# Seventy identity products in TensorE's first gaps instead of twenty-four, in the bank of the second MLP's sum

## The chip, the cores and the metric

The kernel runs on one core of a Trainium2 chip. The metric is the device time of one execution in microseconds (us), as the median of several runs. The engines are called PE (TensorE), DVE (VectorE), ACT (ScalarE), POOL (GpSimd) and SP (SyncE, which issues the DMAs here).

## The reference

12288 queries of 128 channels attend to 768 keys, which are 4x4 averages of `kv` times `w_sr` and serve as values too. Two MLPs with 2048 hidden channels follow.

```python
kv_pool = kv.reshape(B, H // r, r, W // r, r, C).mean(axis=(2, 4))
k = v = kv_pool.reshape(B, -1, C) @ w_sr
a = softmax(q @ k.T / sqrt(C));  x = a @ v
h = x @ w_in;  x = (relu(h) ** 2) @ w_out
h = x @ w_in2
P = a[0] + a[1]*h + a[2]*h**2 + a[3]*h**3
Q = 1 + |b[0]|*|h| + |b[1]|*h**2
out = (P / (Q + 1e-6)) @ w_out2
```

## The kernel before, in words

The queries are cut into 25 blocks: one of 384 columns, 22 of 512, one of 384 and one of 256. Each block goes through three stages, and the stages of several blocks overlap.

- **Setup.** SP loads `kv` in 16 pieces; POOL (L486) and DVE (L482) sum them into pooled keys. PE projects them in two halves (L507 for the keys, L522 for the values); ACT (L511) and DVE (L515) split the projected keys into a high and a low part. The weights arrive as 64-bit words. DVE decodes each piece in four steps (L574, L582, L587, L592), and ACT and POOL split it.
- **Attention.** For each 128 queries PE makes the scores in six passes (L679), DVE takes the minimum, ACT the exponential, POOL the division (L697). PE transposes the result (L720), ACT and DVE split it, and PE multiplies by the values (L749 to L753).
- **First MLP.** The block's input is split into `xh` and `xl` (L779 or L782, and L785). For each of 16 hidden tiles PE makes three passes (L805 to L807, on `w0h` and `w0l`), ACT or DVE takes the ReLU (L847, L850), ACT or POOL the square, and PE adds to the block's sum `y1` (L819, or L823 to L825, on `w0o`, `w0oh`, `w0ol`). At the end `y1` is split into `yh` and `yl` (L779 or L782, and L785).
- **Second MLP.** Hidden tiles go in pairs, eight pairs a block. PE makes three passes for each tile (L805 to L807, on `w1h` and `w1l`). Then a chain of elementwise steps: ACT takes the absolute value (L944) and a square (L958), DVE a product for each tile (L960), POOL or ACT the denominator (L947 and L949, or L952), ACT a logarithm and an exponential (L969, L970), DVE three steps for the pair (L982, L984, L987). Of some pairs the result is split (L997 or L998, and L1000). PE adds to the sum `y2` (L819, or L823 to L825, on `w1o`, `w1oh`, `w1ol`). ACT scales it (L1020) and SP stores it (L1024).

The order of the work is not written out. Every step is given to a planner (`Plan.op`) with an urgency, a cost, the engine or engines that may do it, what it reads and writes, and what storage it takes. `Plan.order` plays all steps through once with these costs. An engine that is free takes the most urgent step that is ready and whose storage is free. The instructions are then issued in that order, on each engine one behind the other. So one more step on one engine can change the order of everything that follows on all of them. The eight banks of PSUM are shared by kinds of tiles, and `caps` says how many of each kind may be held: six of `st` (transposes and projections) and one of `y2`, the second MLP's sum.

The identity products (`warm`, L494 to L501) multiply the 128x128 identity by itself. Nothing reads what they give. They carry an urgency of 1e6, the last of all, so the planner places them where PE has nothing else that is ready.

Of the kernel before, what the change touches and what calls it, by code (L numbers as in the profile page):

```python
# [21 lines left out]
PE, ACT, DVE, POOL, DMA = "PE", "ACT", "DVE", "POOL", "DMA"  # L22
# [45 lines left out]
    rg=1,  # L68
    low=4,
    avs=5,  # L70
    warm=24,
    head=[384],
    tail=[384, 256],
    off=dict(
# [51 lines left out]
    warm=0,  # L126
# [242 lines left out]
def program(ctx, tc, CFG, fast, co, room, wsr, qT, kvT, w1_in, w1_out, w2_in, w2_out, outT):  # L369
# [30 lines left out]
    tiles = {}  # L400
# [5 lines left out]
    def mk(tag, key, shape=None, dtype=None):  # L406
        if tag in caps:
            tiles[key] = psum[:, P.slot[key], :]
            return tiles[key]
        if tag in RINGS:  # L410
            n = turn[tag] = turn.get(tag, -1) + 1
            in_room, at = place_of[tag, n % bufs[tag]]
            t = (room if in_room else more)[:, at:at + RINGS[tag]]
            if dtype:
                t = t.bitcast(dtype)
            if shape:
                size = 1
                for x in shape[1:]:
                    size *= x
                t = t[:, 0:size]  # L420
            else:
                shape = big.get(tag, [128, TM])
            if len(shape) == 3:
                t = t.rearrange("p (a b) -> p a b", b=shape[2])
            tiles[key] = t
            return t
        t = pools[tag].tile(shape or big.get(tag, [128, TM]), dtype or dts.get(tag, F32), tag=tag, name=tag)
        tiles[key] = t
        return t
# [20 lines left out]
    P = Plan(CFG)  # L450
# [25 lines left out]
    for c in range(0, NKEY, KC):  # L476
# [11 lines left out]
        if half(c):  # L488
            P.op(P0, (POOL, c_pool(KC * R2 // 2), add2, 0), wr=[("kv", c)])
        P.op(P0, (DVE, c_dve(KC * R2 // (2 if half(c) else 1)), go2, 0),  # L490
             new=[("const", ("poolT", c))] + ([] if c else [("o", "pool")]), rd=[("kv", c)] + (["pool"] if c else []))
    dma(P0, sizes[0] * 512, load_q(0), new=[("qr", ("qr", 0))])

    def warm(i):  # L494
        def go():
            o = mk("st", "warm") if i == 0 else tiles["warm"]
            nc.tensor.matmul(out=o[:, 0:128], lhsT=ident, rhs=ident, start=True, stop=True)
        return go
    for i in range(CFG["warm"]):
        P.op(1e6, (PE, 260.0, warm(i), 0), new=[("st", "warm")] if i == 0 else [],  # L500
             rd=["ident"], wr=["warm"] if i else [])  # L501

    for h in range(2):
# [575 lines left out]
def attn_moe_moe(  # L1079
# [79 lines left out]
    with tc.If(fits > 0) as branch:  # L1159
        with ExitStack() as c:  # L1160
            co = dict(c=c1(co_f, 0), nd=c1(co_f, 1), e=c1(v, 0), k1=c1(co_f, 2), k2=c1(co_f, 3), dp=c1(co_f, 4),
                      da=c1(co_f, 5), out=c1(co_f, 6))
            program(c, tc, SQUARES, True, co, *args)
    with branch.Else():
        with ExitStack() as c:
            co = dict(a=co_g[:, 0:4], e=c1(co_g, 0), b=co_g[:, 4:6], qc=c1(co_g, 6))
            program(c, tc, TERMS, False, co, *args)
# [39 lines left out]
```

## Time and profile before

| | |
|---|---|
| median of 3 runs | 1488.0 us (1486.13 to 1488.52) |
| the profiled execution | 1486.91 us |
| its span, first to last instruction | 1484.7 us |
| PE busy | 1439.5 us, 97% of the span |
| ACT, DVE, POOL busy | 1393.4, 1386.9, 1334.1 us |
| mean granted clock of PE | 0.989 |

The span is the time between the first and the last instruction in the trace; the execution's own time is 2.2 us longer. The granted clock is a share of full speed: 1.00 is 2.4 GHz and 0.50 is 1.2 GHz. A busy PE is not PE at its peak, since the ends of matmuls are modelled and they overlap.

### The profile page before, as it was taken

Reading aid. Unit: us, or ns where it says so; the run is one execution under the profiler, and the core shown is the slowest. Engines: PE = TensorE matmul, PEld = TensorE weight load, DVE = VectorE, ACT = ScalarE, POOL = GpSimd, SP = SyncE. Lnnn points to the kernel's source line nnn. Section 1 sums busy time; section 2 is a strip of 40 time slices with the busy share of each in tenths; the row PEclk is TensorE's granted clock in tenths of the full one; section 3 lists DMA queues with packets and bytes.
Section 4 is the critical chain, followed back from the end, with each engine's and each line's share of the span. In section 5 each row is a group of like instructions: output and inputs, shape, how many; then the busy total and the mean of one; then the engine's idle time right before and its main releaser. Section 6 shows DMA issues by size and latency. Waiting matters only on the chain.

```text
span 1484.7 us, 18746 instructions
## 1 busy us (share of the span) xinstructions
PE 1439.5 (97%) x5991; PEld 1053.8 (71%) x5991; DVE 1386.9 (93%) x1857; ACT 1393.4 (94%) x2318; POOL 1334.1 (90%) x1021
## 2 busy tenths in 40 slices
PE   5999999999999999999999999999999999999986
PEld 4887767766767777776777777777777777767764
DVE  7999999999999999999999999999989899989998
ACT  3789989999999999999999999999999999999996
POOL 4789999998999899999998997989999999889984
PEclk8999999999999999999999999999999999999998
DMA  7310000000000000000000000000000000000000
GB/s 283 114 36 8 13 0 15 14 2 8 15 8 15 8 3 13 15 8 8 8 15 8 1 15 15 8 8 15 8 8 8 8 13 1 11 5 3 8 8 12
DMA packets 15549, 28.62 MB, mean 19 GB/s; under 512 B 1745, under 2 KB 6737, under 8 KB 15441
## 3 DMA queue, kind: packets, MB, share of 16 engines
q1 hardware_dynamic: 15440, 27.34, 5.5%
q8 instruction: 49, 0.80, 0.2%
q14 instruction: 60, 0.48, 0.1%
HBM read 21.04 MB, written 6.29 MB: 18 GB/s over the span
## 4 chain that ended last, share of the span: by engine, by line
PE 67%; POOL 13%; ACT 8%; DVE 7%; issue 3%; DMA 1%; SPq 0%; POOLq 0%; ACTq 0%; DVEq 0%
PE psum L819 17%; PE psum L805 9%; PE psum L806 8%; PE psum L807 8%; PE psum L679 4%; PE psum L824 4%; POOL room L949 4%; PE psum L825 4%; PE psum L823 4%; PE psum L720 4%; POOL gL L871 3%; POOL room L947 2%; POOL room L856 2%; PE psum L750 1%; PE psum L749 1%
## 5 line engine op out<-in xcount | busy, mean ns | idle before, releaser
L949 POOL TENSOR_TENSOR room<-room 128x1024 f32<-128x1024 f32 (+2 forms) x150 | 348.3, 2322 | 3.6
L871 POOL TENSOR_TENSOR gL<-room,gH 128x512 fp32r<-128x512 f32 (+2 forms) x250 | 313.0, 1262 | 20.8 <-PE psum L824 15.8
L960 DVE SCALAR_TENSOR_TENSOR room<-room,cf,psum 128x512 f32<-128x512 f32 (+2 forms) x400 | 279.5, 720 | 17.4 <-ACT room L958 15.8
L819 PE MATMUL psum<-room,w1o 128*128 128x512 f32 (+2 forms) x600 | 285.2, 583 | 4.0 <-DVE room L987 4.0
L856 POOL TENSOR_TENSOR room<-room 128x512 f32<-128x512 f32 (+2 forms) x261 | 262.3, 1022 | 12.5 <-ACT room L847 6.6
L982 DVE SCALAR_TENSOR_TENSOR room<-room,v,psum 128x1024 f32<-128x1024 f32 (+2 forms) x200 | 246.1, 1232 | 21.2 <-ACT psum L970 19.4
L958 ACT ACTIVATE room<-psum,cf 128x512 f32<-128x512 f32 (+2 forms) x400 | 262.8, 688 | 0.0
L969 ACT ACTIVATE room<-room,cf 128x1024 f32<-128x1024 f32 (+2 forms) x200 | 226.3, 1132 | 25.4 <-POOL room L949 24.8
L984 DVE SCALAR_TENSOR_TENSOR psum<-room,cf,psum 128x1024 f32<-128x1024 f32 (+2 forms) x200 | 247.5, 1238 | 0.0
L987 DVE SCALAR_TENSOR_TENSOR room<-psum,room 128x1024 f32<-128x1024 f32 (+2 forms) x200 | 235.2, 1177 | 3.1
L944 ACT ACTIVATE room<-psum 128x512 f32<-128x512 f32 (+2 forms) x400 | 223.4, 593 | 12.5 <-PE psum L807 6.5
L947 POOL TENSOR_SCALAR room<-room,cf 128x1024 f32<-128x1024 f32 (+2 forms) x150 | 164.7, 1098 | 48.3 <-ACT room L944 36.0
L970 ACT ACTIVATE psum<-room 128x1024 f32<-128x1024 f32 (+2 forms) x200 | 202.7, 1015 | 0.7 <-DVE room L960 0.3
L805 PE MATMUL psum<-yh,w1h 128*128 128x512 f32 (+2 forms) x400 | 191.2, 478 | 4.8 <-DVE room L987 3.5
L805 PE MATMUL psum<-xh,w0h 128*128 128x512 f32 (+2 forms) x400 | 182.8, 457 | 1.6 <-DVE xh L782 1.2
L819 PEld LDWEIGHTS psum<-room,w1o 128*128 128x128 f32 x600 | 111.1, 192 | 63.1 <-issue 42.9
L806 PE MATMUL psum<-xl,w0h 128*128 128x512 f32 (+2 forms) x400 | 153.4, 383 | 1.5 <-DVE xl L785 1.2
L807 PE MATMUL psum<-yh,w1l 128*128 128x512 f32 (+2 forms) x400 | 154.2, 386 | 0.0
L806 PE MATMUL psum<-yl,w1h 128*128 128x512 f32 (+2 forms) x400 | 153.9, 385 | 0.0
L807 PE MATMUL psum<-xh,w0l 128*128 128x512 f32 (+2 forms) x400 | 153.6, 384 | 0.0
L847 ACT ACTIVATE room<-psum 128x512 f32<-128x512 f32 (+2 forms) x255 | 148.3, 601 | 5.1 <-PE psum L807 3.2
L865 ACT ACTIVATE gH<-room 128x512 fp32r<-128x512 f32 (+2 forms) x250 | 149.8, 632 | 2.9 <-POOL room L856 2.6
(126 smaller groups left out, 3124.4 us busy)
## 6 DMA issues: line engine op xcount, KB each, us to landing
room<-in_kv_dram SPq DMA_DIRECT2D x16, 384.0 KB, 7.8
room<-in_q_dram SPq DMA_DIRECT2D x22, 256.0 KB, 2.6
out_dram<-room SPq DMA_DIRECT2D x22, 256.0 KB, 2.0
room<-in_moe_w_in_dram SPq DMA_DIRECT2D x8, 512.0 KB, 4.6
room<-in_moe_w_out_dram SPq DMA_DIRECT2D x16, 256.0 KB, 2.7
room<-in_q_dram SPq DMA_DIRECT2D x2, 192.0 KB, 4.7
out_dram<-room SPq DMA_DIRECT2D x2, 192.0 KB, 1.9
room<-in_q_dram SPq DMA_DIRECT2D x1, 128.0 KB, 2.0
```

The costliest lines, as they stand in the source:

```text
L805: nc.tensor.matmul(out=out, lhsT=w_hi[m][:, sl], rhs=hi, start=True, stop=False)
L806: nc.tensor.matmul(out=out, lhsT=w_hi[m][:, sl], rhs=lo, start=False, stop=False)
L807: nc.tensor.matmul(out=out, lhsT=w_lo[m][:, sl], rhs=hi, start=False, stop=True)
L819: nc.tensor.matmul(out=o, lhsT=w_o[m][:, place[m][fi], :], rhs=rhs(), start=first, stop=last)
L856: nc.gpsimd.tensor_tensor(out=G(), in0=G(), in1=G(), op=ALU.mult)
L871: nc.gpsimd.tensor_tensor(out=mk("gL", gl)[:, :T], in0=G(), in1=f(tiles[gh][:, :T]), op=ALU.subtract)
L949: one("qp", POOL, c_pool, lambda v: nc.gpsimd.tensor_tensor(out=v(ku), in0=v(ku), in1=v(uu), op=ALU.mult), None, [uu], [ku])
L958: one("sP", ACT, ptr(c_actp), lambda v: act(out=v(zz), in_=v(hh), func=AF.Square, bias=co["c"]), "Z", [hh])
L960: one("z3", DVE, ptr(c_dve), lambda v: stt(out=v(zz), in0=v(zz), scalar=co["nd"], in1=v(hh), op0=ALU.subtract, op1=ALU.mult), None, [hh], ...
L982: one("g0", DVE, ptr(c_dve), lambda v: stt(out=v(zz), in0=v(zz), scalar=e0, in1=v(yy), op0=ALU.add, op1=ALU.mult), None, [yy], [zz])
L984: one("tt", DVE, c_dl, lambda v: stt(out=v(yy), in0=v(ku), scalar=dl, in1=v(yy), op0=ALU.add, op1=ALU.mult), None, [ku], [yy])
L987: one("g2", DVE, c_dve, lambda v: stt(out=v(g_), in0=v(yy), scalar=2.0, in1=v(zz), op0=ALU.subtract, op1=ALU.mult, reverse0=True), None, [ ...
```

## The change

The table entry `warm` goes from 24 to 70, and the first of these products takes its bank as a `y2` tile, no longer as a `st` tile. The bank is held until the last of them is done.

```diff
-    warm=24,
+    warm=70,
...
     def warm(i):
         def go():
-            o = mk("st", "warm") if i == 0 else tiles["warm"]
+            o = mk("y2", "warm") if i == 0 else tiles["warm"]
             nc.tensor.matmul(out=o[:, 0:128], lhsT=ident, rhs=ident, start=True, stop=True)
         return go
     for i in range(CFG["warm"]):
-        P.op(1e6, (PE, 260.0, warm(i), 0), new=[("st", "warm")] if i == 0 else [],
+        P.op(1e6, (PE, 260.0, warm(i), 0), new=[("y2", "warm")] if i == 0 else [],
              rd=["ident"], wr=["warm"] if i else [])
```

The planner's order moves with it, in three places that matter below. The first is PE's start, up to the second projection (L497 are the identity products, L507 and L522 the projections; lines with a minus are the order before).

```order
-L497 MATMUL psum<-ident 128x128 x24
+L497 MATMUL psum<-ident 128x128 x35
 L507 MATMUL psum<-room,wsr 128x384
 L522 MATMUL psum<-wsr,room 128x128 x3
+L497 MATMUL psum<-ident 128x128 x15
 L507 MATMUL psum<-room,wsr 128x384
 L522 MATMUL psum<-wsr,room 128x128 x3
```

Eleven more products stand ahead of the first projection, and 15 between the first and the second.

The second place is PE from the end of the third tile's scores to the first product with the values, as it stands now (L679 are the scores, L720 the transposes).

```order
L679 MATMUL psum<-k_hi,ql 128x384 x2
L497 MATMUL psum<-ident 128x128 x9
L679 MATMUL psum<-k_hi,qh 128x384 x2
L679 MATMUL psum<-k_lo,qh 128x384 x2
L679 MATMUL psum<-k_hi,ql 128x384 x2
L497 MATMUL psum<-ident 128x128 x6
L720 MATMUL psum<-ident,room 128x128 x18
L497 MATMUL psum<-ident 128x128 x2
L749 MATMUL psum<-aH,v_hi 128x384
L750 MATMUL psum<-aL,v_hi 128x384
L751 MATMUL psum<-aH,v_lo 128x384
L497 MATMUL psum<-ident 128x128
```

Nine products stand between the third and the fourth tile's scores, six ahead of the transposes and three around the first product with the values; two more stand right behind the second projection. Before, there was none in any of these places.

The third place is the end of the program on DVE, around the last split of a first MLP's sum (`yl`, 256 columns wide, L785): after it nothing is left but second MLPs. Before:

```order
L960 SCALAR_TENSOR_TENSOR room<-room,cf,psum 128x384 x2
L987 SCALAR_TENSOR_TENSOR room<-psum,room 128x2x384
L850 TENSOR_SCALAR room<-psum 128x256
L998 CAST mH<-room 128x2x384
L982 SCALAR_TENSOR_TENSOR room<-room,v,psum 128x2x384
L984 SCALAR_TENSOR_TENSOR psum<-room,cf,psum 128x2x384
L987 SCALAR_TENSOR_TENSOR room<-psum,room 128x2x384
L982 SCALAR_TENSOR_TENSOR room<-room,v,psum 128x2x384
L960 SCALAR_TENSOR_TENSOR room<-room,cf,psum 128x384 x2
L785 TENSOR_TENSOR yl<-psum,yh 128x256
L984 SCALAR_TENSOR_TENSOR psum<-room,cf,psum 128x2x384
```

And now:

```order
L984 SCALAR_TENSOR_TENSOR psum<-room,cf,psum 128x1024
L960 SCALAR_TENSOR_TENSOR room<-room,cf,psum 128x384
L987 SCALAR_TENSOR_TENSOR room<-psum,room 128x1024
L960 SCALAR_TENSOR_TENSOR room<-room,cf,psum 128x384
L982 SCALAR_TENSOR_TENSOR room<-room,v,psum 128x2x384
L984 SCALAR_TENSOR_TENSOR psum<-room,cf,psum 128x2x384
L960 SCALAR_TENSOR_TENSOR room<-room,cf,psum 128x384
L987 SCALAR_TENSOR_TENSOR room<-psum,room 128x2x384
L960 SCALAR_TENSOR_TENSOR room<-room,cf,psum 128x384
L782 CAST yh<-psum 128x256
L785 TENSOR_TENSOR yl<-psum,yh 128x256
L982 SCALAR_TENSOR_TENSOR room<-room,v,psum 128x2x384
```

The split has moved ahead past second-MLP work of the block of 384 columns. Of that block, DVE had behind the split 5 instructions of L982, 6 of L984, 6 of L987 and 8 of L960, and none of L998; now it has 7, 7, 7, 10 and one. The eight pairs of the block of 256 columns stand behind it in both. On PE, behind the last product on `w0o`, 8 hidden tiles of the 384 block's second MLP were left (L805 to L807 on `w1h` and `w1l`), and now 10.

## Rows read from the trace of the kernel before

**Rows 1.** The page, part 1: busy time, share of the span and instructions of each engine.

```profile
PE 1439.5 (97%) x5991; PEld 1053.8 (71%) x5991; DVE 1386.9 (93%) x1857; ACT 1393.4 (94%) x2318; POOL 1334.1 (90%) x1021
```

**Rows 2.** The page, part 4: the chain that ended last, by engine.

```profile
PE 67%; POOL 13%; ACT 8%; DVE 7%; issue 3%; DMA 1%; SPq 0%; POOLq 0%; ACTq 0%; DVEq 0%
```

**Rows 3.** Busy time by stretch; columns: length, each engine's busy us, clock, DMA share, GB/s.

```profile
100.00:1400.00 1300.00, 1291.53 (x5294) 934.27 (x5293) 1221.48 (x1547) 1256.94 (x2040) 1210.29 (x891) 1.00 0.03 9
1433.20:1480.00 46.80, 33.80 (x129) 24.45 (x128) 43.91 (x68) 38.20 (x79) 24.92 (x22) 0.82 0.02 5
```

**Rows 4.** The same view for the start (order: PE, PEld, DVE, ACT, POOL, clock).

```profile
19.10:25.80 6.70, 2.67 (x9) 2.06 (x9) 6.41 (x11) 2.17 (x4) 1.91 (x2) 0.51 1.02 388
26.00:32.70 6.70, 4.39 (x24) 3.73 (x23) 6.60 (x14) 5.07 (x11) 2.77 (x3) 0.99 0.76 250
32.80:39.50 6.70, 5.69 (x23) 4.57 (x23) 6.56 (x15) 4.33 (x9) 6.35 (x7) 0.51 0.39 117
39.60:47.60 8.00, 6.45 (x33) 5.51 (x32) 7.11 (x18) 4.76 (x10) 3.52 (x4) 0.99 0.21 58
```

**Rows 5.** The same view, the identity products' passes alone (PE, PEld, clock).

```profile
8.20:12.00 3.80, 3.77 (x17) 3.77 (x18) 1.00 1.03 415
12.00:15.70 3.70, 3.70 (x33) 3.66 (x31) 1.00 1.04 404
```

**Rows 6.** Timeline of PE at the start: start us, us, line, operation, [idle before, releaser].

```profile
15.69 0.81 PE L507 MATMUL psum<-room,wsr 128*128 128x384 f32 x2
...
23.14 1.65 PE L507 MATMUL psum<-room,wsr 128*128 128x384 f32 x2 [5.97 <-DVE room L482]
...
25.72 0.78 PE L679 MATMUL psum<-k_hi,qh 128*128 128x384 f32 x2
...
31.19 0.62 PE L679 MATMUL psum<-k_hi,qh 128*128 128x384 f32 x2 [1.91 <-ACT qh L655]
...
35.23 3.67 PE L720 MATMUL psum<-ident,room 128*128 128x128 f32 x16 [0.41 <-POOL room L697]
...
47.64 0.41 PE L805 MATMUL psum<-xh,w0h 128*128 128x384 f32 x1 [1.16 <-DVE xh L782]
...
52.46 1.47 PE L720 MATMUL psum<-ident,room 128*128 128x128 f32 x12
```

**Rows 7.** Timelines of ACT and DVE at the start: the keys' high and low parts.

```profile
16.60 0.49 ACT L511 ACTIVATE k_hi<-psum 128x384 fp32r<-128x384 f32 x1 [14.59 <-PE psum L507]
...
19.34 0.55 DVE L515 SCALAR_TENSOR_TENSOR k_lo<-psum,k_hi 128x384 fp32r<-128x384 f32 x1
...
25.77 0.55 DVE L515 SCALAR_TENSOR_TENSOR k_lo<-psum,k_hi 128x384 fp32r<-128x384 f32 x1
```

**Rows 8.** Timeline of DVE at the end, the last `yl` and two of L982 behind it.

```profile
1433.17 0.42 DVE L785 TENSOR_TENSOR yl<-psum,yh 128x256 fp32r<-128x256 f32 x1
...
1436.60 1.00 DVE L982 SCALAR_TENSOR_TENSOR room<-room,v,psum 128x768 f32<-128x768 f32 x1
...
1451.99 1.00 DVE L982 SCALAR_TENSOR_TENSOR room<-room,v,psum 128x768 f32<-128x768 f32 x1
```

**Rows 9.** Groups of DVE by shape, from 1421 us on: count | busy us, mean ns.

```profile
L984 DVE SCALAR_TENSOR_TENSOR psum<-room,cf,psum 128x768 f32<-128x768 f32 x8 | 8.1, 1016 | 0.0
L960 DVE SCALAR_TENSOR_TENSOR room<-room,cf,psum 128x384 f32<-128x384 f32 x14 | 8.1, 609 | 0.8 <-ACT room L958 0.8
L982 DVE SCALAR_TENSOR_TENSOR room<-room,v,psum 128x768 f32<-128x768 f32 x8 | 8.1, 1009 | 0.9 <-ACT psum L970 0.6
L987 DVE SCALAR_TENSOR_TENSOR room<-psum,room 128x768 f32<-128x768 f32 x8 | 7.6, 954 | 0.2
...
L998 DVE CAST mH<-room 128x768 fp32r<-128x768 f32 x1 | 0.8, 750 | 0.0
```

**Rows 10.** Timeline of PE at the end: the two tiles of one pair, 384 columns.

```profile
1428.26 0.34 PE L805 MATMUL psum<-yh,w1h 128*128 128x384 f32 x1
...
1428.78 0.33 PE L805 MATMUL psum<-yh,w1h 128*128 128x384 f32 x1
```

## The prediction

> **What bounds the kernel now.** I read the busy shares first: PE has 97% of the span, but the other three have 90 to 94% [rows 1], so no engine has much room. The chain that ended last says the same: PE holds 67% of it, and POOL, ACT and DVE the other large parts [rows 2]. So I went by stretches. From 100 to 1400 us PE is busy 1291.53 of 1300 us at full clock: that stretch is PE's, and 8.5 us are idle in all [rows 3]. Two stretches are not PE's. At the start DVE is the full engine: from 19.1 to 39.5 us it is busy 6.41, 6.60 and 6.56 of 6.70 us each, while PE has 2.67 to 5.69 [rows 4]. At the end, from 1433.2 us, PE is busy 33.80 of 46.80 us and DVE 43.91 [rows 3]: the first MLPs are over, and DVE sets the pace of what is left. The timelines then show what stands at the edges of these two stretches [rows 6, 7, 8].
>
> **The start: 46 products more.** Price of one: each is two passes; 17 passes took 3.77 us up to 12.0 us, and then 33 took 3.70 us [rows 5] (a pass that straddles an edge counts on both sides). So a pass was 0.222 us at first and 0.112 us later, and a product 0.444 or 0.224 us. (The printed clock is 1.00 in both; the doubled passes say that the first stretch ran at 1.2 GHz.) The first 35 products are 70 passes: 17 slow ones to 12.0 us, 53 x 0.112 = 5.9 us more, so they end at 17.9. The first projection began at 15.69 [rows 6] and now begins 2.2 us later. Who waits for it is the first low part of the keys, which DVE made at 19.34, behind 12 of its 16 pooling steps [rows 7]. ACT began on the projected keys 0.9 us after the projection's start, at 16.60, and took 0.5 us [rows 7]; 17.9 + 1.4 = 19.3. So the cover is used up to the last tenth, and I cost it at nothing; each further 0.1 us would stop DVE. The 15 products behind it follow the first projection's passes, about 1.3 us at full clock (half of what the second one took at half clock, below): 17.9 + 1.3 + 15 x 0.224 = 22.6 us, ahead of the second projection's 23.14, which waited for DVE's last pooling step [rows 6]. Cost nothing; 0.5 us of that cover are left.
>
> What they give: PE no longer stands still, so the second projection should run at 2.4 GHz. It took 2.6 us (23.14 to 25.72) at a granted 0.51 [rows 4, 6]; 1.3 would be saved. But the scores behind it need the second low part, which DVE began at 25.77 behind three decoding steps [rows 7]. So this gain is nothing: DVE is late next. The nine products, 2.0 us, fill an idle 1.91 us [rows 6]; the six, 1.3 us, end before the third tile's division, which released the transposes at 35.23. The 16 transposes behind it took 3.67 us at 0.51; twelve at full clock took 1.47 [rows 4, 6], so sixteen would take 1.96, 1.7 us less. Upper end for the whole start: all PE work of the two slow stretches at double speed, (2.67 + 5.69) / 2 = 4.2 us [rows 4]. But DVE works through its own list at nearly no rest: from 26.0 to 47.6 us it was idle 0.10 + 0.14 + 0.89 = 1.1 us [rows 4], and the first MLP's start at 47.64 waited for DVE [rows 6]. So a faster PE can give 0 to 1.1 us. I take **-0.6 us**, the middle, since no row is nearer.
>
> The Trainium skill, "TensorE: Matmul & The Clock Gate", section "Part 1: The HAM clock gate", says that the throttled state is the default and that activity releases it. The trace agrees: the clock was 0.51 after PE had stood still, and full once it was busy. By that rule alone the products would give the whole 4.2 us, and the sum below would be 3.6 us lower.
>
> The bank costs nothing: the `y2` tile is wanted only when block 0's second MLP adds up, far behind the last identity product, and all six `st` tiles are now free for others.
>
> **The middle.** Order differs on every engine from here on. The same useful passes run in a stretch that PE fills; what can change is its 8.5 us of idle time [rows 3]. Bounds -8.5 (none left) and +8.5 (twice as much). I take 0: it is the same planner with the same costs.
>
> **The end.** The mark is the last `yl` on DVE, 1433.17 us [rows 8]. Up to there PE sets the time; it has two hidden tiles of 384 columns less to do ahead of it, each 0.52 us [rows 10]: **-1.0 us**. Behind it DVE has more. In busy time: 2 x 1.01 (L982) + 1.02 + 0.95 + 2 x 0.61 (L960) + 0.75 (L998) = 6.0 us [rows 9], or 5.4 us, since each such row begins some 0.08 us before the one ahead of it ends (1436.60 + 1.00 against the next start at 1437.52). If DVE's idle time of 46.80 - 43.91 = 2.9 us [rows 3] took some of that in, 2.5 us would be left: the low end. The pace of pairs is the other measure: four lay between the L982 at 1436.60 and the one at 1451.99 [rows 8], 3.85 us each. Seven L982 stand behind the mark instead of five: 7.7 us, and with the added L998 8.4, the high end. I take **+7.7**: five steps on ACT and POOL lie between a pair's first passes and its L982, so a pair that has not reached it when PE runs dry costs its pace and not its DVE time alone. The clock in this stretch was 0.82 already [rows 3]; PE waits there anyway.
>
> **Sum.** 1486.9 - 0.6 - 1.0 + 7.7 = 1493.0 us on the scale of the profiled execution. The median of the runs lies 1.1 us above that one, so I forecast **1494.0 us**, 6 us or 0.4% above the median before. About 0.2%, 3 us, is what a measurement of this kernel can tell from no change: faster means under 1485.0 and slower over 1491.0.
>
> **Rivals.**
> - *The clock decides (faster).* PE at full speed brings the first MLP forward by the whole 4.2 us [rows 4], that lead is carried through the stretch that PE fills, and the added DVE work at the end fits into its idle 2.9 us and the earlier mark. Time: 1488.0 - 4.2 + (2.5 - 1.0) = 1485.3, and under 1485 with a little less idle time in the middle. It decides if DVE's list at the start gets shorter ahead of the first MLP; for it speaks the wait of 1.16 us there [rows 6], against it DVE's 1.1 us of rest. The skill's rule above is this case's mechanism. Chance 0.08.
> - *They cancel.* The low end of the tail, 2.5 - 1.0, less the 1.1 us of the start: 1488.4 us. For it speaks that DVE's stretches are never wholly full. Chance 0.20.
> - *The products come too late.* If the clock is not raised at 12 us, 50 products at 0.444 us and the projections at half speed end at 8.2 + 22.2 + 2.6 = 33.0 us, against 23.14 [rows 6]: DVE's decoding hides little of 10 us, so 1494 + 8 = 1502. Against it: the passes doubled their pace at 12 us with the same products [rows 5]. It decides from a delay of 0.5 us on. Chance 0.05.
> - That the change does not do what it says I give no share: the order shows all 70 products ahead of the first MLP.
>
> **How the numbers follow.** The forecast has 0.67 and these cases 0.33. The forecast's own bounds are 1488.0 - 1.1 - 1.0 + 2.5 = 1488.4 to 1488.0 - 0 - 1.0 + 8.4 = 1495.4 from start and tail, and up to 8.5 us either way from the middle, of which I allow about 5 above and 1 below. So the range is 1487.5 to 1500.5; it holds the forecast and the cancelling case, and leaves out the clock case, the late products and the far ends of the middle. Slower by over 0.2%: 0.67 + 0.05 = 0.72. Within: 0.20. Faster: 0.08.
>
> **What would show it.** Right: passes of 0.112 us for L497 from about 12 us on and a granted clock of 1.00 up to some 1430 us; the second projection still near 23.1 us; the first MLP's first pass between 46.5 and 47.6; the last `yl` of 256 columns within 2 or 3 us of 1433, and about 59 us from there to the end of the span instead of 1484.7 - 1433.2 = 51.5. Wrong: a first pass at 44 us, the last `yl` ahead of 1428, or a tail of 51 to 54 us behind it; or, the other way, idle time well over 8.5 us between 100 and 1400.

## The result, and the profile after

The changed kernel takes 1497.3 us (median of six runs, 1496.6 to 1498.5), the kernel before on the same chip 1487.2: a ratio of 1.0068 with a 95% interval of 1.0055 to 1.0081. It is slower by 10.1 us, where +6 was forecast. The spans of the two profiled executions lie 11.8 us apart, since that of the changed kernel is the slowest of its six. The page of the changed kernel, span 1496.5 us, the lines that answer to [rows 1, 2] and the granted clock in 40 slices:

```profile
PE 1451.1 (97%) x6083; PEld 1061.4 (71%) x6083; DVE 1384.4 (93%) x1858; ACT 1397.0 (93%) x2316; POOL 1335.1 (89%) x1022
...
PEclk9999999999999999999999999999999999999987
...
PE 71%; POOL 11%; DVE 7%; ACT 6%; issue 3%; DMA 1%; SPq 0%; ACTq 0%; POOLq 0%; DVEq 0%
```

The shares look as before. PE has 92 passes more, and DVE is busy 2.5 us less although the span is 11.8 us longer. The start by stretches (columns as in [rows 4]):

```profile
19.10:25.80 6.70, 4.92 (x40) 4.46 (x39) 5.11 (x9) 1.82 (x5) 1.75 (x2) 1.00 0.94 364
26.00:32.70 6.70, 5.98 (x42) 5.66 (x42) 6.63 (x13) 4.46 (x11) 3.39 (x3) 1.00 0.85 278
32.80:39.50 6.70, 5.99 (x46) 5.33 (x45) 6.56 (x17) 5.44 (x13) 5.38 (x7) 1.00 0.38 117
```

The granted clock is 1.00 where it was 0.51. Yet DVE, the full engine of this place, has 5.11 us of work in the first stretch in place of 6.41. Its timeline says why (start us, us, line, operation, [idle before, releaser]):

```profile
19.24 0.56 DVE L515 SCALAR_TENSOR_TENSOR k_lo<-psum,k_hi 128x384 fp32r<-128x384 f32 x1
19.77 2.27 DVE L482 TENSOR_REDUCE room<-room 128x48 f32<-128x768 f32 x3
23.41 0.95 DVE L482 TENSOR_REDUCE room<-room 128x48 f32<-128x768 f32 x1 [1.36 <-DMA room<-in_kv_dram]
24.28 0.55 DVE L537 SCALAR_TENSOR_TENSOR v_lo<-psum,v_hi 128x384 fp32r<-128x384 f32 x1
25.02 0.69 DVE L574 TENSOR_SCALAR psum<-room 128x512 int32<-128x512 int32 x1 [0.19 <-DMA room<-in_moe_w_in_dram]
...
27.08 0.55 DVE L515 SCALAR_TENSOR_TENSOR k_lo<-psum,k_hi 128x384 fp32r<-128x384 f32 x1
```

The first `k_lo` is on time (19.34 before). Then DVE waits 1.36 us for the last piece of `kv`, and the second `k_lo` stands at 27.08, not at 25.77. PE in the same execution:

```profile
8.04 9.93 PE L497 MATMUL psum<-ident 128*128 128x128 f32 x70 [8.04 <-POOL ident masks.py:199]
...
46.63 0.44 PE L805 MATMUL psum<-xh,w0h 128*128 128x384 f32 x1 [0.58 <-ACT xh L779]
```

The first 35 products end at 17.97 us, and the first MLP begins 1.0 us earlier than in [rows 6]. So the loss lies later. PE by stretches shows where it appears, first in the kernel before, then in the changed one (length, busy us, passes, granted clock, DMA share, GB/s):

```profile
60.00:200.00 140.00, 139.51 (x629) 1.00 0.08 25
200.00:700.00 500.00, 494.59 (x1999) 1.00 0.03 10
700.00:1400.00 700.00, 697.43 (x2863) 1.00 0.03 9
1400.00:1484.70 84.70, 67.36 (x294) 0.89 0.03 9
```

```profile
60.00:200.00 140.00, 136.54 (x617) 1.00 0.09 27
200.00:700.00 500.00, 495.88 (x1995) 1.00 0.03 10
700.00:1400.00 700.00, 697.47 (x2865) 1.00 0.03 9
1400.00:1496.50 96.50, 73.61 (x306) 0.86 0.02 8
```

Length less busy time is PE's idle time: 0.5, 5.4, 2.6 and 17.3 us before, 3.5, 4.1, 2.5 and 22.9 now. At 1400 us the changed kernel has 12 passes more to do (306 against 294), and the part behind 1400 us is 11.8 us longer. That is 5.6 us more idle time, 12 x 0.229 = 2.7 us for the passes left over (0.229 is 67.36 / 294), and 3.5 us because 306 passes take 0.2406 us each and not 0.2291, at a granted 0.86. The split goes by mean values and is rough: nine of the 12 passes are 512 columns wide, which take longer than the mean. The slowing shows within one kind of pass too: the 24 of L819 on `w1o` with 384 columns took 637 ns each, and 542 before. The last split of a first MLP's sum, and PE's and DVE's waits behind it (us in total, times, longest), answer to [rows 8]:

```profile
1434.38 0.42 DVE L785 TENSOR_TENSOR yl<-psum,yh 128x256 fp32r<-128x256 f32 x1
```

```profile
PE psum L819 <- DVE room L987: 6.8, 5, 1.9
PE psum L824 <- POOL mL L1000: 5.8, 4, 3.0
PE psum L823 <- DVE room L960: 2.3, 1, 2.3
```

```profile
DVE room L960 <- ACT room L958: 4.3, 5, 1.4
```

The mark is 1.2 us later, and 62.1 us lie behind it where 51.5 lay. In the kernel before these waits were 4.0, 3.9, none, and 0.7 us. One other fell, that of L805 for L987, from 3.5 to 1.6 us; all waits of PE behind the mark add up to 16.7 us, and to 12.9 before. The chain between the engines runs dry for longer, and the granted clock behind the mark is 0.78 where it was 0.82.

The idle time between 60 and 200 us has names too. PE is busy 8.27 of 10 us between 70 and 80 us, and 18.26 of 20 between 180 and 200, and full in between:

```profile
PE psum L805 <- DVE room L987: 1.1, 1, 1.1
PE psum L806 <- DVE xl L785: 0.9, 1, 0.9
PE psum L805 <- DVE sm L693: 0.8, 1, 0.8
```

In the kernel before the longest wait there is 0.3 us.

### The profile page after: what moved, and what is told of

It is laid out like the page before. It is cut to its first block, busy times and chain, and to the rows that moved or that the text cites. A ratio compares the mean times of both kernels' runs of the same rounds, so it can differ in the third digit from the quotient of the medians.

```text
span 1496.5 us, 18939 instructions
## 1 busy us (share of the span) xinstructions
PE 1451.1 (97%) x6083; PEld 1061.4 (71%) x6083; DVE 1384.4 (93%) x1858; ACT 1397.0 (93%) x2316; POOL 1335.1 (89%) x1022
## 4 chain that ended last, share of the span: by engine, by line
PE 71%; POOL 11%; DVE 7%; ACT 6%; issue 3%; DMA 1%; SPq 0%; ACTq 0%; POOLq 0%; DVEq 0%
PE psum L819 19%; PE psum L805 9%; PE psum L807 9%; PE psum L806 9%; PE psum L679 5%; PE psum L824 4%; PE psum L825 4%; PE psum L823 4%; POOL room L949 3%; PE psum L720 3%; POOL gL L871 2%; PE psum L749 2%; PE psum L751 2%; PE psum L750 2%; POOL room L947 1%
## 5 line engine op out<-in xcount | busy, mean ns | idle before, releaser
L819 PE MATMUL psum<-room,w1o 128*128 128x512 f32 (+2 forms) x600 | 287.8, 586 | 6.9 <-DVE room L987 6.9
L960 DVE SCALAR_TENSOR_TENSOR room<-room,cf,psum 128x512 f32<-128x512 f32 (+2 forms) x400 | 279.6, 719 | 13.3 <-ACT room L958 11.3
L856 POOL TENSOR_TENSOR room<-room 128x512 f32<-128x512 f32 (+2 forms) x265 | 266.4, 1023 | 17.7 <-ACT room L847 6.9
L982 DVE SCALAR_TENSOR_TENSOR room<-room,v,psum 128x1024 f32<-128x1024 f32 (+2 forms) x200 | 246.1, 1232 | 28.5 <-ACT psum L970 27.2
L984 DVE SCALAR_TENSOR_TENSOR psum<-room,cf,psum 128x1024 f32<-128x1024 f32 (+2 forms) x200 | 247.1, 1237 | 0.0
L969 ACT ACTIVATE room<-room,cf 128x1024 f32<-128x1024 f32 (+2 forms) x200 | 225.1, 1126 | 19.3 <-POOL room L949 18.1
L944 ACT ACTIVATE room<-psum 128x512 f32<-128x512 f32 (+2 forms) x400 | 223.0, 587 | 17.9 <-PE psum L807 12.4
L987 DVE SCALAR_TENSOR_TENSOR room<-psum,room 128x1024 f32<-128x1024 f32 (+2 forms) x200 | 235.0, 1175 | 2.7
L805 PE MATMUL psum<-yh,w1h 128*128 128x512 f32 (+2 forms) x400 | 188.6, 471 | 3.4 <-DVE room L987 3.1
L805 PE MATMUL psum<-xh,w0h 128*128 128x512 f32 (+2 forms) x400 | 182.0, 455 | 2.8 <-ACT room L686 1.0
L819 PEld LDWEIGHTS psum<-room,w1o 128*128 128x128 f32 x600 | 111.8, 194 | 65.5 <-issue 43.3
L807 PE MATMUL psum<-yh,w1l 128*128 128x512 f32 (+2 forms) x400 | 154.5, 386 | 0.0
L807 PE MATMUL psum<-xh,w0l 128*128 128x512 f32 (+2 forms) x400 | 153.6, 384 | 0.0
```

The source lines that it names most:

```text
L805: nc.tensor.matmul(out=out, lhsT=w_hi[m][:, sl], rhs=hi, start=True, stop=False)
L807: nc.tensor.matmul(out=out, lhsT=w_lo[m][:, sl], rhs=hi, start=False, stop=True)
L819: nc.tensor.matmul(out=o, lhsT=w_o[m][:, place[m][fi], :], rhs=rhs(), start=first, stop=last)
L856: nc.gpsimd.tensor_tensor(out=G(), in0=G(), in1=G(), op=ALU.mult)
L960: one("z3", DVE, ptr(c_dve), lambda v: stt(out=v(zz), in0=v(zz), scalar=co["nd"], in1=v(hh), op0=ALU.subtract, op1=ALU.mult), None, [hh], ...
L982: one("g0", DVE, ptr(c_dve), lambda v: stt(out=v(zz), in0=v(zz), scalar=e0, in1=v(yy), op0=ALU.add, op1=ALU.mult), None, [yy], [zz])
```

## The experiments

### Is it the order, or are it the products and their bank?

Theory A: the planner, given 46 more steps, orders everything else in another way, and that order is worse. Its rivals: the products' own time and their bank, or the clock. Five runs, of which the first two each change one thing and keep the other. The first puts 43 products into the old order.

```diff
+    more_at = {}
+    if fast:
+        w = P.slot["warm"]
+        for key, n, bank in ((("kp", 0), 11, w), (("kp", 1), 15, w), (("sc", 0, 0, 0), 2, w),
+                             (("sc", 1, 0, 0), 9, 7), (("st", 0, 0), 6, 7)):
+            more_at[P.keys[key]["users"][0]] = (n, bank)
...
-        for _, _, emit in order:
+        for _, i, emit in order:
+            for _ in range(more_at.get(i, (0, 0))[0]):
+                nc.tensor.matmul(out=psum[:, more_at[i][1], 0:128], lhsT=ident, rhs=ident, start=True, stop=True)
```

> The kernel before, with its own order of every instruction kept, and 43 more identity products put into TensorE's stream by hand at five places of the start (11 ahead of the first projection, 15 ahead of the second, 2 ahead of the first scores, 9 ahead of the fourth scores, 6 ahead of the first transposes). So 67 products, with no other instruction moved. Theory A (the other order of all the work costs the 10 us, the products nothing): the first MLP's first pass near 46.6 us in place of 47.64, no later loss, ratio 0.9990 to 1.0005, so 1485.7 to 1488.0 us. Rival B (the products themselves hold up VectorE's first keys and the projections, and the delay is carried to the end): ratio 1.003 to 1.007, with the first MLP's pass after 48 us. Rival C (the granted clock or the power later in the program answers for it): first MLP early, but passes in the middle longer, ratio above 1.002.

Measured: 0.9998 (0.9989 to 1.0007), 1486.95 us against 1487.25. The clock is up at the start as in the changed kernel, and nothing is lost or won. The first MLP did not come earlier, as Theory A had it: 47.95 us. The end is that of the kernel before: the mark at 1433.21, 51.3 us behind it.

```profile
19.10:25.80 6.70, 5.88 (x46) 5.17 (x45) 5.04 (x9) 1.96 (x5) 1.83 (x2) 1.00 0.95 367
...
32.80:39.50 6.70, 5.62 (x43) 4.80 (x42) 6.53 (x15) 4.65 (x11) 6.41 (x8) 1.00 0.37 118
```

The second run keeps the new order and leaves 46 products out:

```diff
             o = mk("y2", "warm") if i == 0 else tiles["warm"]
+            if i >= 24:
+                return
```

> The changed kernel with its order of every instruction kept, but its identity products 25 to 70 left out: 24 products as before, in the bank of the second MLP's sum. Theory A (the order costs the time): ratio 1.006 to 1.009 to the kernel before, 1496 to 1500 us, the time behind the last layer norm's mark near 62 us as in the changed kernel. Rival B (the products cost it): ratio 0.999 to 1.001, and 51 to 53 us behind the mark.

Measured: 1.0056 (1.0041 to 1.0071), 1495.7 us. The order alone brings 8.4 us of the 10.1, a little less than the 1.006 expected; the intervals of the two kernels overlap, so that no cost of the 46 products is clear here. The same three waits stand between 60 and 200 us, with 1.1, 0.9 and 0.8 us. The mark ("the last layer norm's mark" of the expectation; the kernel has no layer norm, it is the last `yl`) is at 1434.28 and 59.8 us lie behind it. Here the first MLP began at 45.62 us, earlier than in any other run, and the kernel is among the slow ones.

The next two ask whether it is this change, or any other count of products:

```diff
-    warm=24,
+    warm=8,
```

> The kernel before with 8 identity products in place of 24, in the old bank, ordered anew. Theory A (any count that orders the rest otherwise moves the time, in either direction): a ratio that differs from 1 by more than 0.003, as likely above 1.006 as the changed kernel, though it has fewer products; the loss lies far behind the products, most of it behind 1400 us. Rival B (the products' own time decides): 0.998 to 1.0005, 16 passes of 0.11 to 0.22 us fewer, so up to 3 us off the start and nothing else. Rival C (the products are what warms the clock): the passes of the first projections at 0.222 us and the loss, 1 to 4 us, all ahead of 50 us.

Measured: 1.0154 (1.0138 to 1.0169), 1510.2 us. With sixteen products fewer the kernel is 23 us slower. The first MLP starts at 50.58 us, 2.9 later than before, and most of the loss comes behind that:

```profile
60.00:200.00 140.00, 136.70 (x609) 1.00 0.09 25
200.00:700.00 500.00, 491.05 (x1977) 1.00 0.03 10
700.00:1400.00 700.00, 697.40 (x2851) 1.00 0.03 9
1400.00:1508.50 108.50, 84.34 (x360) 0.88 0.02 7
```

It has the pattern of the changed kernel, larger: 3.3 and 9.0 us idle up to 700 us, 66 passes more left at 1400, and 24.2 us idle behind that.

> 70 identity products as in the changed kernel, but in the old bank (that of the statistics), so the count alone without the bank. Theory A (the count sets the order, the bank nothing): an order much like the changed kernel's, but not the same, ratio 1.004 to 1.011. Rival B (the bank of the second MLP's sum, busy later, is what holds the start up): ratio 0.999 to 1.002.

```diff
-    warm=24,
+    warm=70,
```

Measured: 1.0124 (1.0108 to 1.0139), 1505.9 us: the same 70 products in the old bank are 8.6 us slower than in the new one. So the bank moves the time as well, and Theory A's upper bound was too low. Whether the old bank does so by the order alone, this run does not tell; that the new one need not cost anything, the next run does. (The old bank, `st`, is that of transposes and projections, not of statistics.)

The strongest test, the fifth run, is the changed kernel with its products and its bank, and one due number of the planner's table raised by 2 (that of the first MLP's ReLU):

```diff
-        mh2=-266.25, mh1=-79.25, sc=-10.0, tr=0.75, nr=-368.25, g2=7.0, ex=-137.5, kk=-177.25, rl=-4.75,
+        mh2=-266.25, mh1=-79.25, sc=-10.0, tr=0.75, nr=-368.25, g2=7.0, ex=-137.5, kk=-177.25, rl=-2.75,
```

> The changed kernel (70 identity products, bank of the second MLP's sum) with one number of the planner's table changed: the relu of the first MLP's hidden tiles (L847, L856's line of work) is due 2 of the planner's units later. It has the same 70 products at the same places of the start; the order of the rest is another. Theory A (the order of the rest decides, and the changed kernel drew a bad one): 1486 to 1490 us, ratio 0.999 to 1.002 to the kernel before, with 12 L982 behind the last `yl` and some 48 us from it to the end. Rival B (the products or their bank cost the time): as the changed kernel, 1.005 to 1.008.

Measured: 0.9999 (0.9989 to 1.0008), 1486.9 us. The 10 us are gone. The work, the products, their places and the early first MLP (46.54 us) are as in the changed kernel; the idle times of PE are 0.7, 4.9, 1.6 and 17.3 us, and 290 passes are left at 1400:

```profile
60.00:200.00 140.00, 139.29 (x626) 1.00 0.09 27
200.00:700.00 500.00, 495.14 (x2001) 1.00 0.03 10
700.00:1400.00 700.00, 698.39 (x2862) 1.00 0.03 9
1400.00:1484.30 84.30, 67.00 (x290) 0.90 0.03 9
```

### Does a pair behind the mark cost its pace?

This is the term of the forecast for the end. Two runs move the last block's first MLP in the kernel before, and nothing ahead of the end:

```diff
-                mlp1(b, fi, 16 * b + fi - LEAD1 - CFG["ramp1"] * b)
+                mlp1(b, fi, 16 * b + fi - LEAD1 - CFG["ramp1"] * b - (1 if b == NB - 1 else 0))
```

> The kernel before (24 identity products) with one number changed: the last block's first MLP is due one step earlier. The order stays as it was up to some 1340 us; behind the last `yl` on VectorE stand 11 of the L982 instead of 13. Theory T (the term of the forecast for the end: each pair behind the mark costs its pace of 3.85 us): 43.8 us behind the mark in place of 51.5, the mark at most 2 us later, so 1480 to 1483 us, ratio 0.995 to 0.997. Rival M (the mark only moves: TensorE does the two pairs ahead of it, and it comes later by what the part behind it is shorter): ratio 0.999 to 1.002.

> The kernel before with the last block's first MLP due four steps earlier: 14 of the L982 behind the last `yl` instead of 13. Theory T (pairs behind the mark): 55 us behind the mark, the mark up to 2 us earlier, 1489 to 1492 us, ratio 1.001 to 1.003. Rival M (the mark only moves): 0.999 to 1.001, the mark some 4 us earlier. Theory A (any other order of the end is a draw of its own) allows either sign, up to 0.4%.

(The second has a 4 in place of the 1.) Measured: 0.9999 (0.9990 to 1.0009) and 1.0014 (1.0004 to 1.0024). The mark of the first (span 1485.7 us), then of the second (1487.6 us):

```profile
1440.31 0.42 DVE L785 TENSOR_TENSOR yl<-psum,yh 128x256 fp32r<-128x256 f32 x1
```

```profile
1431.26 0.42 DVE L785 TENSOR_TENSOR yl<-psum,yh 128x256 fp32r<-128x256 f32 x1
```

With two pairs fewer behind it 45.4 us are left, 6.1 less, but the mark is 7.1 us later: nothing won, as Rival M has it. With one L982 more 56.3 are left, 4.8 more, and the mark is only 1.9 us earlier: 1.8 us lost by the medians, as Theory T has it. So the term is borne out by one of the two. Counting pairs gives the length behind the mark (43.8 and 55 were expected), but the mark moves with them, by more or by less. In the run with the one number, 12 of the L982 stand behind a mark at 1439.82, and 44.5 us follow: again the total of the kernel before. The 70 products in the old bank have 14 of the L982 behind their mark, as many as the second run here, and take 17 us longer; that mark is at 1444.30. So the count of pairs behind the mark does not tell the time of a kernel.

### What do the early products cost, and how?

In the runs with many products ahead of the second projection the first pieces of the weights land late, and in the changed kernel the last piece of `kv` too. The DMA issues from 14 to 27 us (size, median us from issue to landing), before, then after:

```profile
room<-in_moe_w_in_dram SPq DMA_DIRECT2D x4, 512.0 KB, 7.8
...
room<-in_kv_dram SPq DMA_DIRECT2D x1, 384.0 KB, 7.8
```

```profile
room<-in_moe_w_in_dram SPq DMA_DIRECT2D x4, 512.0 KB, 9.2
...
room<-in_kv_dram SPq DMA_DIRECT2D x1, 384.0 KB, 9.5
```

What else differs there is one transfer of instructions (queue, packets, MB, share of 16 engines), at 28 to 36 us before and at 20 to 22 us after:

```profile
q8 instruction: 1, 0.02, 0.8%
```

```profile
q8 instruction: 1, 0.02, 3.5%
```

3.5% of 16 engines over 2 us is 1.1 us of one DMA engine, in a stretch in which all are full. Theory I is that the added instructions bring it forward to there. First, the old order with 17 products more, all behind 24 us (the insertion of the first run, without its first two places):

```diff
-        for key, n, bank in ((("kp", 0), 11, w), (("kp", 1), 15, w), (("sc", 0, 0, 0), 2, w),
+        for key, n, bank in ((("sc", 0, 0, 0), 2, w),
```

> The order of the kernel before, with only 17 products more, all behind 24 us: 2 ahead of the first scores, 9 ahead of the fourth, 6 ahead of the first transposes. In the runs with 67 and 70 products the last pieces that VectorE reads at the start land 1.3 us later than with 24, and a transfer of instructions of 0.02 MB lies at 20 to 22 us instead of 28 to 36. Theory I (more instructions ahead of 22 us bring that transfer forward, into the loads): here the first decoding step (L574) starts at 23.7 us as in the kernel before, and the transfer lies behind 26 us. Rival (the granted clock or TensorE's business delays the loads): the step at 25.0. In either case the time is that of the kernel before, ratio 0.9985 to 1.0005; the first MLP's pass between 46.3 and 47.7 us.

Measured: 0.9985 (0.9976 to 0.9995), 1485.2 us, 2 us faster than the kernel before and at the lower edge of what was expected. The transfer is at 28 to 36 us and the decoding step on time:

```profile
23.68 0.69 DVE L574 TENSOR_SCALAR psum<-room 128x512 int32<-128x512 int32 x1 [0.17 <-DMA room<-in_moe_w_in_dram]
```

So the later products gain something. The clock is up in the second of the slow stretches, and nothing else was moved:

```profile
32.80:39.50 6.70, 5.61 (x40) 1.00 0.38 117
```

The first MLP begins at 47.13, 0.5 us earlier than in the kernel before, and the mark is at 1431.77, 1.4 us earlier. That the clock is what gains this is likely, but no run separates it from the rest.

That run has a quieter PE too. The next one keeps PE as busy with a quarter of the instructions:

```diff
-        for key, n, bank in ((("kp", 0), 11, w), (("kp", 1), 15, w), (("sc", 0, 0, 0), 2, w),
+        for key, n, bank in ((("kp", 0), 3, w), (("kp", 1), 4, w), (("sc", 0, 0, 0), 2, w),
...
+                wide = more_at[i][0] in (3, 4)
...
+                                 rhs=ident[:, None, :].broadcast_to([128, 4, 128]) if wide else ident,
```

> The run with 67 products in the old order once more, but the 26 added ahead of the two projections are replaced by 7 of 512 columns each (the identity read four times over), 3 ahead of the first and 4 ahead of the second: about the same busy time of TensorE at the same places and the same clock, with 7 products' instructions in place of 26. Theory I (the number of instructions ahead of 22 us brings a transfer of instructions into the loads): the transfer behind 24 us, the first decoding step (L574) at 23.6 to 23.8 us, the first MLP's pass 0.6 to 1.3 us earlier than the 47.95 of the 67, ratio 0.9978 to 0.9998. Rival P (a busy TensorE, or its clock, holds the loads up): the step at 25.0 us and the ratio 0.999 to 1.0007, as with the 67.

Measured: 0.9988 (0.9979 to 0.9997), 1484.9 us against 1486.7 in that series. PE is busy 6.53 of 6.70 us from 19.1 us on at a clock of 1.00, the transfer is at 28 to 36 us, and the weights land in time:

```profile
room<-in_moe_w_in_dram SPq DMA_DIRECT2D x4, 512.0 KB, 7.8
```

```profile
20.58 0.56 DVE L515 SCALAR_TENSOR_TENSOR k_lo<-psum,k_hi 128x384 fp32r<-128x384 f32 x1 [1.28 <-ACT k_hi L511]
21.06 3.12 DVE L482 TENSOR_REDUCE room<-room 128x48 f32<-128x768 f32 x4
24.09 0.55 DVE L537 SCALAR_TENSOR_TENSOR v_lo<-psum,v_hi 128x384 fp32r<-128x384 f32 x1
24.56 0.68 DVE L574 TENSOR_SCALAR psum<-room 128x512 int32<-128x512 int32 x1
```

Rival P falls: PE is as busy, and no load is late or waited for. The step itself stood at 24.56 and not at 23.7, for a reason not expected: in this execution the first 24 products took 8.53 us (7.48 in the run with 67), the first projection came at 19.15, and DVE waited 1.28 us for ACT. The first MLP began at 47.46.

The last three runs look for a version that beats both kernels: the table with the one number, with products 25 to 50 left out, and a table whose due times were searched anew, with all 70 and without those 26.

```diff
             o = mk("y2", "warm") if i == 0 else tiles["warm"]
+            if 24 <= i < 50:
+                return
```

> The kernel with 70 products and the relu due 2 units later, its order kept, but the identity products 25 to 50 left out: the 26 that stand between the first 24 and the first scores. So 44 products: 24 at the front, 20 behind 24 us. Theory I (the 26 products bring the transfer of instructions into the loads and hold up the first low part of the keys): the transfer back behind 26 us, the first decoding step at 23.7 us in place of 24.93, the first MLP's pass 0.7 to 1.2 us earlier than 46.54, the span 0.5 to 1.5 us shorter than with all 70: ratio 0.9985 to 0.9996 to the kernel before. Rival (what is gained at the start is lost again on the way, as in the run with the 67 products in the old order): ratio 0.9995 to 1.0005.

> The changed kernel with all 70 products and the planner's table searched anew (numbers of due times and of engine choice; the work itself is the same). Theory A (the order of the rest is what decides, and the count of products only sets where one starts): 1484 to 1487.5 us, ratio 0.998 to 1.0005, first MLP near 46.5 us, 11 L982 behind the last `yl`. Rival B (the bank or the products cost some us whatever the order): 1.002 or more.

```diff
-        mh2=-266.25, mh1=-79.25, sc=-10.0, tr=0.75, nr=-368.25, g2=7.0, ex=-137.5, kk=-177.25, rl=-4.75,
+        mh2=-272.0, mh1=-150.0, sc=-9.75, tr=0.75, nr=-452.25, g2=7.25, ex=-104.5, kk=-154.75, rl=-2.5,
...
```

> The kernel with the table searched anew, its order kept, but products 25 to 50 left out (44 remain). Theory I: the first decoding step at 23.7 us, the span 0.5 to 1.5 us shorter than that with all 70; ratio 0.9965 to 0.9995 to the kernel before, so the fastest of the study. Rival (nothing carried on): as the one with 70.

Measured: 0.9984 (0.9975 to 0.9993), 1.0002 (0.9993 to 1.0011) and 0.9986 (0.9977 to 0.9995); 1485.2, 1487.9 and 1485.0 us. Without the 26 products the transfer lies behind 28 us in both, the first decoding step is at 23.60 and 23.62, and each order gains some 0.0015, about 2 us. Not all of that lies inside the span: the execution is 2.6 us longer than its span in the 67 products and in the one number with 70, 2.2 in the kernel before, and 1.8 in the four fastest versions and in the searched 70 (medians). Against the kernels before of their series, the spans gain 0.6 us from the 67 to the wide products, 0.9 to the 17 later ones, 1.0 in the order with the one number, and 3.0 in the searched order. What the time outside the span is, no run tells. The searched table gave nothing beyond the one number. The best versions, in three different orders, all end at 1485 us: 24 products at the front, no further 128-column ones until 24 us, and 17 to 20 behind.

## Why the prediction was right

The sign and the range held, the range because 5 us had been allowed above for the middle: the mark, with the start in it, and the length behind it each came out some 3 us above the sum. The terms, one by one:

- **Price of the products: right.** 70 passes forecast to end at 17.9 us ended at 17.97, and the first `k_lo` was not held up. To the tenth this is luck: in the four other kernels with 35 products there they ended at 18.1 to 19.3 us, and the first `k_lo` waited 0.31 us in one and 1.09 in another.
- **The cover of the 15 products behind it: wrong.** "Cost nothing; 0.5 us of that cover are left" counted PE and DVE and no DMA. The loads came 1.3 us late, with the transfer of instructions among them, and the second projection began at 24.42, not near 23.1. The pairs of runs with and without the early products give some 2 us for the kernel, of which 0.6 to 3.0 within the span. The rule of the Trainium skill that the prediction weighed (the page "TensorE: Matmul & The Clock Gate", "Part 1: The HAM clock gate") is that activity releases the throttle. The trace agrees, with 1.00 granted where it was 0.51; the 4.2 us that the prediction worked out for this rule alone did not come.
- **The start, -0.6 us: near in size, not for its reason.** The first MLP came 1.0 us earlier. The clock alone did not give that: with the same products in the old order it came at 47.95, and with the new order and 24 products at 45.62. It is the order that starts it 2 us earlier and the products that take 1 us back. Nor was it worth anything in the new order: the kernel with the earliest first MLP lost 8.4 us. The reason itself, a faster PE worth 0 to 1.1 us, fits the 17 later products in the old order, with 0.5 us at the first MLP; the early products undid it.
- **The middle, 0 with bounds of 8.5 either way: off by 1.6 us of idle time, and the stretch was cut wrong.** From 100 to 1400 us PE is busy 1291.61 us, as before [rows 3]. The loss lies ahead of that: 3.0 us more idle time between 60 and 200 us, of which 1.7 lie between 70 and 80 and 1.3 come back by 700.
- **The mark, -1.0 us: wrong.** It came 1.2 us later. PE had two tiles less to do ahead of it, but it had stood idle 1.6 us longer between 60 and 1400 us. That makes 0.6; the rest of the 1.2 stays open.
- **The end, +7.7 us: mis-sized, and its reason carries only in part.** Behind the mark it was +10.6. Of the two runs that move the last block, one bears the pace of a pair out and one does not, since pairs behind a mark move the mark as well; no time can be summed from them alone. What the 11.8 us behind 1400 us consist of is PE's idle time, in which it waits for DVE and POOL (5.6), passes left over from the loss ahead (2.7) and slower passes (3.5), with a granted clock of 0.86 in place of 0.89. The prediction left the slower passes at nothing, since PE waits there anyway.

Of the rivals, "the clock decides" is refuted: from 19 us on the clock was 1.00 throughout the start in six kernels whose times lie between 1484.9 and 1505.9 us. "They cancel" fell with 10.1 us, and "the products come too late" with the end of the first 35 at 17.97. That an order is a draw of its own, in either direction, was not among them, and it is the main cause: "it is the same planner with the same costs" was taken for a zero. The seven other orders of the same useful work that ran here lie 0 to 23 us above the kernel before. Why this planner's orders are so far apart stays open. The trace names the waits that make the 3 us between 60 and 200 us, but no run isolated the step of the order behind them.

## What to carry to other kernels

Where a planner sets the order of all engines, any added step, even one that nobody waits for, can draw a new order; test it by adding the step at emission with the order held, and by holding the new order without the step, before crediting or blaming the step itself. A clock raised at a place where another engine is full gave nothing or 2 us of 1487 here, depending on what was added along with it. Filler for PE costs instructions as well as time: while the loads that the start waits for were under way, 26 narrow products cost what seven wide ones of the same busy time did not.

## What was not expected of the hardware

- **A transfer of instructions among full loads.** Where the 0.02 MB of instructions came at 20 to 22 us, while the DMA engines were full, the weights' pieces of 512 KB took 9.0 to 9.2 us, where they took 7.8 to 8.1 without it. In four kernels with the transfer there (the changed one, the 67, the 70 in the old bank, the searched 70) the first decoding step stood at 24.96 to 25.03 us; in eight that have none there up to 28 us, at 23.60 to 23.77. In a fifth, the one number with 70 products, it came at 22 to 23 us: the pieces took 8.9 us and the step stood at 24.93, but DVE was late there by itself (the first `k_lo` at 20.58) and waited only 0.29 us for the load. The run with the wide products separates it from a busy PE. That the one engine that carries it is what the loads wait for is an inference. It fits that in the changed kernel the mean busy share of the DMA engines fell to 0.41 between 25.0 and 25.5 us (0.98 before), while SP still waited, until 25.38, for a piece of `q` to land.
- **The front's first 24 products are not repeatable.** The same 48 passes from about 8 us on took 7.02 to 8.53 us in nine kernels. PE's pace goes from 7 to 11 passes a us near 11 us in the kernel with 7.02, and near 14 us in the one with 8.53. The Trainium skill ("TensorE: Matmul & The Clock Gate", "Part 1: The HAM clock gate") says that the number of cold matmuls differs between runs. The traces agree. A cover of some tenths of a us behind them, as the prediction used, is not a cover.
